# Second network in groups of 512 rows across experts, its outputs with channels on partitions

## The chip, the cores and the metric

The kernel runs on one core of a Trainium2 chip. The core has five engines with instruction streams of their own: TensorE (PE in the profile, matmuls), VectorE (DVE), ScalarE (ACT), GpSimd (POOL) and SyncE (SP, which issues most DMA transfers). They wait for each other by semaphores. The metric is the device time of one execution in microseconds; 707.64 before is the median of three runs (706.99 to 707.85).

## The reference

Three parts follow each other. Attention over 4 x 3072 positions with 256 channels gives 12288 rows. A mixture of experts sends each row to the one of eight experts with the highest gate, of which each takes at most `capacity` = 384 rows; the rest give zeros. A second network runs over all rows; the rows that no expert kept are zero going in and zero coming out, so only 8 x 384 = 3072 rows need it. The last two parts decide here:

```python
    h = np.maximum(np.einsum('ecd,edf->ecf', disp, w1), 0.0)   # 8 experts, 384 rows, 256 -> 1024
    y = np.einsum('ecf,efd->ecd', h, w2)                       # 1024 -> 256
    ...
            out[i] = gate_w[i] * y[expert_idx[i], pos[i]]
    ...
    h = x @ w_in                                               # 256 -> 2048
    g = np.where(h > 0.0, h, alpha * (np.exp(np.minimum(h, 0.0)) - 1.0))
    return (g @ w_out).astype(np.float32)                      # 2048 -> 256
```

## The kernel before

Every float32 product is made of three matmuls on rounded halves, high times high, low times high, high times low (`triples`, L127). A halving is one ACT instruction that rounds (`rounded`, L117) and one on DVE that takes the remainder (`rest`, L120). Weights of the experts come as raw float32 tiles of 1 MB, one for each layer of an expert (`load_w`, L145), and are halved in four pieces of 512 columns per layer (`split_w`, L231); a raw tile takes the next expert's load when its last piece is halved.

The experts' own network is `layer1` (L265, six matmuls of 384 columns for a tile of 128 hidden units, eight tiles), `hidden` (L277, ACT and DVE) and `layer2` (L286, six of 384). Expert 0 is done ahead of `feed_forward` (L1714). The second network then runs expert by expert: for expert e and each of 16 tiles f of 128 hidden units there is a step with `layer3` (six matmuls of 384), the ELU (class `Elu`: three ACT instructions at L1748 to L1750, two DVE sums at L1753 and L1756, then the halving) and `layer4` (three matmuls of 512 and three of 256, in which the activations are the stationary operand, so that the outputs come with rows on partitions, in three PSUM banks o0 to o2). After its 16 tiles, `finish` adds the two halves of each bank, and GpSimd writes the rows to their tokens.

PE, ACT, DVE and SP take their instructions in the order in which the code is written. In it `layer4` follows `layer3` by a lag of four products. The lag grows by one at six tiles of the last expert but one (`RAMP`), to ten, so that at the end PE has ten products to do while the last ELU is made. Layers 1 and 2 of expert n + 1 are placed among the 16 steps of expert n by the table `plan`, as are the weight halvings, loads, turns of the dispatched rows and zero fills. Expert 1's first layer1 comes right before the loop, the others in its steps 0 to 12, layer2 in its steps 4 to 13.

The ELU's tiles m, x and t have two buffers each, g three, the halves gh and gl ten. Dispatched rows come in "squares": 32 by 32 blocks, loaded in pieces of 128 bytes from DRAM so that DVE's 32 by 32 transpose gives whole turned tiles (`load_squares`, L178; `turn`, L236).

Of the kernel before, what the change touches and what calls it, by code (L numbers as in the profile page):

```python
# [19 lines left out]
P = 128  # L20
# [11 lines left out]
def tile_attn_moe_ffn(  # L32
# [28 lines left out]
    HALVED = 2  # L61
    assert D == 256 and E == 8 and DQ == 64 and cap % P == 0 and S % QA == 0
# [115 lines left out]
    def load_squares(e, to=None):  # L178

        if to is None:  # L180
            t = turns(1 + e % 2, 3, [P, ND, cap], F32, "squares")
            to = [t[:, d, :] for d in range(ND)]
# [18 lines left out]
    def load_toks(e):  # L201

        toks[e] = turns(1 + e % 3, 4, [P, CT, 1], F32, "toks")
# [32 lines left out]
    def turn(e, d, pool, to=None):  # L236
# [7 lines left out]
        else:  # L244
            t = to
            if t is None:
                t = pool.tile([P, cap], F32, tag="sq", name="sq", bufs=2)
# [29 lines left out]
    def hidden(e, f, ps):  # L277
        hi = hp.tile([P, cap], F32R, tag="hh", name="hh")
        lo = hp.tile([P, cap], F32R, tag="hl", name="hl")
# [1434 lines left out]
    def feed_forward(its, reach):  # L1714
        wp = its.enter_context(tc.tile_pool(name="wp", bufs=1))
        pools.append(its.enter_context(tc.tile_pool(name="dp2", bufs=1)))
        gp = its.enter_context(tc.tile_pool(name="gp", bufs=10))
        op = its.enter_context(tc.tile_pool(name="op", bufs=3))

        gs, os_ = {}, {}  # L1720

        def layer3(e, f):
            xh, xl = x2[e]
            ps = psum([P, cap], "h2")
            c = slice(f % 2 * P, (f % 2 + 1) * P)
            w = win[f // 2]
# [6 lines left out]
        class Elu:  # L1733

            def __init__(self, e, f, ps):
                self.ps = ps
                self.m, self.x, self.t = (
                    gp.tile([P, cap], F32, tag=n, name=n, bufs=2) for n in "mxt"  # L1740
                )
                self.g = gp.tile([P, cap], F32, tag="g", name="g", bufs=3)
                self.hi, self.lo = gs[e, f] = tuple(
                    gp.tile([P, cap], F32R, tag=n, name=n) for n in ("gh", "gl")
                )
# [6 lines left out]
            def sum(self):  # L1752
                nc.vector.scalar_tensor_tensor(  # L1753
                    out=self.t, in0=self.x, scalar=1.0, in1=self.t, op0=ALU.add, op1=ALU.mult
                )
                nc.vector.scalar_tensor_tensor(  # L1756
                    out=self.g, in0=self.ps, scalar=0.0, in1=self.t, op0=ALU.max, op1=ALU.add
                )

            def round(self):  # L1760
                rounded(self.hi, self.g)

            def rest(self):
                rest(self.lo, self.g, self.hi)

        def layer4(e, f, js=range(CT)):
            if f == 0:
# [22 lines left out]
        def finish(e, js=range(CT)):  # L1790
            for j in js:
                o = os_[e][j]
                t = op.tile([P, D], F32, tag="t", name="ot")
                nc.scalar.activation(out=t, in_=o[:, D:2 * D], func=ACTF.Copy)
                y = op.tile([P, D], F32, tag="y", name="oy")
                nc.vector.tensor_tensor(out=y, in0=o[:, 0:D], in1=t, op=ALU.add)  # L1796
                put = nc.gpsimd.indirect_dma_start(  # L1797
                    out=out[0:reach, :],
                    out_offset=bass.IndirectOffsetOnAxis(
                        ap=toks[e][:, j, :].bitcast(I32), axis=0  # L1800
                    ),
                    in_=y,
                    in_offset=None,
# [174 lines left out]
```

## Time and profile before

| | |
|---|---|
| profiled run | 707.44 us, its span 705.7 us |
| busy share of PE, DVE, ACT | 99%, 80%, 80% |
| granted TensorE clock, mean | 0.998 |
| second network with the layers of experts 1 to 7 | 314.2 to 700.5 us |
| last matmul, last output write issued | 700.13 us, 701.67 us |

Times in rows are microseconds from the start of the span, unless marked ns. A matmul's duration is longer than its distance to the next one, since matmuls are pipelined: distances from start to start give the throughput. The same holds for ACT and DVE where an instruction doesn't depend on the one ahead of it. "[0.21 <-PE h]" behind a row is idle time of that engine before it and what ended it.

### The profile page before, as it was taken

To read this page: it belongs to the slowest core of one execution; us is meant where nothing else is said; L and a number is where in the kernel's file an instruction comes from. 1 tells how busy PE (TensorE), PEld (TensorE's weight loads), DVE (VectorE), ACT (ScalarE), POOL (GpSimd) and SP (SyncE) were. 2 spreads that over 40 slices of the span, in tenths; PEclk is the share of its full clock that TensorE was granted. 3 is DMA by queue.
4 is the path that set the end of the run, shared out by engine and by line. 5 is a ranking of instruction groups with operands and counts; after the bars stand their busy time and mean duration, and the time that the engine had idled before them with its cause. 6 is when DMAs were issued, how large, how long until landed. Compare 5 with 4: busy or idle time off the path is not lost. (4 is left out here: it accounts for less than half of the span.)

```text
span 705.7 us, 11738 instructions
## 1 busy us (share of the span) xinstructions
PE 698.1 (99%) x3773; PEld 634.0 (90%) x3773; DVE 567.5 (80%) x1191; ACT 565.0 (80%) x1176; POOL 87.1 (12%) x143
## 2 busy tenths in 40 slices
PE   9999999999999999999999999999999999999997
PEld 6888888888888789999999999999999999999996
DVE  7879899898998968688797777777777777787782
ACT  7999989888775789759787777787777877787892
POOL 1003422303130201010001001001001001001011
PEclk9999999999999999999999999999999999999999
DMA  7878999989898864459821602603505406200000
GB/s 178 267 228 222 280 230 226 247 177 215 201 183 136 177 205 133 138 182 293 259 45 31 202 1 73 181 1 119 136 1 148 108 8 193 76 1 23 1 16 31
DMA packets 204595, 98.29 MB, mean 139 GB/s; under 512 B 158389, under 2 KB 193245, under 8 KB 204016
## 3 DMA queue, kind: packets, MB, share of 16 engines
q1 hardware_dynamic: 200016, 84.19, 47.1%
q0 software_dynamic: 4512, 13.31, 5.2%
q8 instruction: 30, 0.49, 0.3%
q14 instruction: 37, 0.30, 0.1%
HBM read 58.31 MB, written 38.03 MB: 137 GB/s over the span
## 5 line engine op out<-in xcount | busy, mean ns | idle before, releaser
L1778 PE MATMUL o<-wout,gh 128*128 128x512 f32 x384 | 139.2, 394 | 0.0
L1753 DVE SCALAR_TENSOR_TENSOR t<-x,t 128x384 f32<-128x384 f32 x128 | 71.5, 559 | 82.6 <-ACT t L1750 81.3
L1748 ACT ACTIVATE m<-h 128x384 f32<-128x384 f32 x128 | 62.7, 490 | 67.9 <-PE h L132 67.3
L1782 PE MATMUL o<-wout,gl 128*128 128x256 f32 x384 | 106.9, 280 | 0.0
L1130 ACT ACTIVATE own<-s 128x512 f32<-128x512 f32 (+1 forms) x123 | 68.4, 557 | 26.7 <-PE s L656 20.2
L129 PE MATMUL h<-xh,win 128*128 128x384 f32 x256 | 85.8, 335 | 0.0
L130 PE MATMUL h<-xh,win 128*128 128x384 f32 x256 | 85.5, 334 | 0.0
L1778 PEld LDWEIGHTS o<-wout,gh 128*128 128x128 f32 x384 | 71.8, 187 | 11.2
L1136 ACT ACTIVATE own<-own 128x512 f32<-128x512 f32 (+1 forms) x123 | 73.7, 599 | 2.7
L1756 DVE SCALAR_TENSOR_TENSOR g<-h,t 128x384 f32<-128x384 f32 x128 | 71.3, 557 | 4.4
L1782 PEld LDWEIGHTS o<-wout,gl 128*128 128x128 f32 x384 | 72.7, 189 | 0.2
L1749 ACT ACTIVATE x<-m 128x384 f32<-128x384 f32 x128 | 67.3, 526 | 4.1
L121 DVE TENSOR_TENSOR gl<-g,gh 128x384 fp32r<-128x384 f32 x128 | 69.9, 546 | 0.2 <-ACT gh L118 0.2
L118 ACT ACTIVATE gh<-g 128x384 fp32r<-128x384 f32 x128 | 65.2, 509 | 0.9 <-DVE g L1756 0.9
L132 PE MATMUL h<-xl,win 128*128 128x384 f32 x256 | 65.6, 337 | 0.0
L1750 ACT ACTIVATE t<-m 128x384 f32<-128x384 f32 x128 | 65.0, 508 | 0.0
L132 PE MATMUL acc<-ownr,vs 128*128 128x512 f32 (+1 forms) x204 | 59.0, 370 | 0.0
L1797 POOL DMA_INDIRECT out_dram<-oy,toks x21 | 21.4, 1020 | 295.8 <-DVE oy L1796 180.9
L129 PE MATMUL acc<-ownr,vs 128*128 128x512 f32 (+1 forms) x144 | 52.4, 367 | 0.0
L129 PEld LDWEIGHTS h<-xh,win 128*128 128x128 f32 x256 | 48.0, 188 | 4.7
L130 PE MATMUL acc<-ownr,vs 128*128 128x512 f32 (+1 forms) x144 | 51.8, 363 | 0.0
L130 PEld LDWEIGHTS h<-xh,win 128*128 128x128 f32 x256 | 48.0, 187 | 0.3
(169 smaller groups left out, 1704.1 us busy)
## 6 DMA issues: line engine op xcount, KB each, us to landing
raw<-in_moe_w_dram SPq DMA_DIRECT2D x16, 1024.0 KB
out_dram<-fill SPq DMA_DIRECT2D x32, 384.0 KB
own<-mir SPq DMA_DIRECT2D x180, 64.0 KB
mir<-own SPq DMA_DIRECT2D x36, 192.0 KB
vr<-in_v_dram SPq DMA_DIRECT2D x24, 256.0 KB
raw<-in_moe_w_in_dram SPq DMA_DIRECT2D x4, 1024.0 KB
raw<-in_moe_w_out_dram SPq DMA_DIRECT2D x4, 1024.0 KB
win<-win_d SPq DMA_DIRECT2D x8, 512.0 KB
```

Of the source, the lines that this page charges most:

```text
L118: nc.scalar.activation(out=out, in_=src, func=func)
L121: nc.vector.tensor_tensor(out=out, in0=src, in1=fp(hi), op=ALU.subtract)
L129: nc.tensor.matmul(out=ps, lhsT=hi, rhs=rh, start=first, stop=False)
L130: nc.tensor.matmul(out=ps, lhsT=lo, rhs=rh, start=False, stop=False)
L132: nc.tensor.matmul(out=ps, lhsT=hi, rhs=rl, start=False, stop=last)
L1130: nc.scalar.activation(out=s["a"][:, :nq], in_=s.pop("ps"), func=ACTF.Relu)
L1136: nc.scalar.activation(out=a, in_=a, func=ACTF.Square)
L1749: nc.scalar.activation(out=self.x, in_=self.m, func=ACTF.Exp, scale=-1.0)
L1753: nc.vector.scalar_tensor_tensor(out=self.t, in0=self.x, scalar=1.0, in1=self.t, op0=ALU.add, op1=ALU.mult)
L1756: nc.vector.scalar_tensor_tensor(out=self.g, in0=self.ps, scalar=0.0, in1=self.t, op0=ALU.max, op1=ALU.add)
L1778: both = lambda: nc.tensor.matmul(out=o, lhsT=hi[:, sl], rhs=w.rearrange("p a d -> p (a d)"), start=(f == 0), stop=(f == NF2 - 1),)
L1782: one = lambda: nc.tensor.matmul(out=o[:, 0:D], lhsT=lo[:, sl], rhs=w[:, 0, :], start=False, stop=False)
```

## The change

The 3072 rows are taken as six groups of 512, across the borders of experts, with 16 tiles each: 96 steps in place of 128. The input of the second network lies in a ring of 1536 columns (`xhr`, `xlr`) into which the outcome of every expert is halved (`settle`; `moved_on` copies expert 0's). `layer3` is six matmuls of 512. In groups 0 to 4 `layer4` is six matmuls of 512, with the weights stationary: outputs with channels on partitions, in one pair of PSUM banks, `ob`. After a group's last tile ACT copies one bank and DVE the other, two transfers write them to DRAM, sixteen read them back as squares, and six and seven steps later DVE turns them and GpSimd writes the rows out. The last group keeps the old form, with four banks.

Since the first group needs expert 1's rows too, expert 1's sixteen layers come before the first step, in a stretch of ten rounds. `layer2` of every expert now has its own bank pair, `yb`. Tiles m and t have one buffer, x three, gh and gl seven, squares one set instead of two. The ramp stands in the last group, at tiles 8, 10, 12 and 14, and uses the tiles of the halved expert weights, which are free by then. The table spreads layers 1 and 2 of experts 2 to 7 to ends at steps 11, 22.67, 34.33, 46, 62 and 78.

```diff
@@ -59,6 +59,8 @@
     CT = cap // P
     QA, QB, QC = 512, 320, 384
     HALVED = 2
+    GR, RING = 512, 4 * cap
+    GBUFS, LAG, RAMP = 7, 4, (8, 10, 12, 14)
...
@@ -1714,15 +1717,48 @@
     def feed_forward(its, reach):
         wp = its.enter_context(tc.tile_pool(name="wp", bufs=1))
         pools.append(its.enter_context(tc.tile_pool(name="dp2", bufs=1)))
-        gp = its.enter_context(tc.tile_pool(name="gp", bufs=10))
-        op = its.enter_context(tc.tile_pool(name="op", bufs=3))
-
-        gs, os_ = {}, {}
-
-        def layer3(e, f):
-            xh, xl = x2[e]
-            ps = psum([P, cap], "h2")
...
+        ring = tuple(xr.tile([P, ND, RING], F32R, name=n) for n in ("xhr", "xlr"))
+        yt, sqr = (
+            [xr.tile([P, 2 * D], F32, name=f"{n}{i}") for i in range(2)] for n in ("yt", "ysq")
+        )
+        back = [dram.tile([D, GR], F32, name=f"back{reach}{i}") for i in range(2)]
+        yb, ob = (
+            [ps_a.tile([P, GR], F32, tag=f"a{d}", name=f"{n}{d}") for d in range(ND)]
+            for n in ("yb", "ob")
+        )
+
...
+        def moved_on():
+            hi, lo = x_of(0)
+            nc.scalar.activation(out=hi, in_=fp(x2[0][0]), func=ACTF.Copy)
+            nc.vector.tensor_copy(out=lo, in_=fp(x2[0][1]))
+
+        def settle(e, ds=range(ND)):
+            hi, lo = x_of(e)
+            for d in ds:
+                split(hi[:, d, :], lo[:, d, :], ys[e][d])
+
+        def bank(e):
+            ys[e] = [t[:, 0:cap] for t in yb]
+
+        def held(e, f, ps):
+            hi, lo = (gp.tile([P, GR], F32R, tag=n, name=n)[:, 0:cap] for n in ("gh", "gl"))
+            hidden(e, f, ps, (hi, lo))
+
+        def layer3(g, f):
+            ps = psum([P, GR], "h2")
             c = slice(f % 2 * P, (f % 2 + 1) * P)
+            x = slice(g * GR % RING, g * GR % RING + GR)
+            xh, xl = (t[:, :, x] for t in ring)
             w = win[f // 2]
             triples(*(
                 (ps, w[:, 0, k, c], w[:, 1, k, c], xh[:, k, :], xl[:, k, :], k == 0, k == ND - 1)
...
-            def __init__(self, e, f, ps):
+            def __init__(self, g, f, ps):
                 self.ps = ps
                 self.m, self.x, self.t = (
-                    gp.tile([P, cap], F32, tag=n, name=n, bufs=2) for n in "mxt"
-                )
-                self.g = gp.tile([P, cap], F32, tag="g", name="g", bufs=3)
-                self.hi, self.lo = gs[e, f] = tuple(
-                    gp.tile([P, cap], F32R, tag=n, name=n) for n in ("gh", "gl")
-                )
+                    gp.tile([P, GR], F32, tag=n, name=n, bufs=b) for n, b in zip("mxt", (1, 3, 1))
+                )
+                if g == NG - 1 and f in RAMP:
+                    i = RAMP.index(f)
+                    t = fixed[("w1", "w2")[i // 2], i % 2].rearrange("p a b c -> p a (b c)")
+                    self.hi, self.lo = t[:, 0, :], t[:, 1, :]
+                else:
+                    self.hi, self.lo = (gp.tile([P, GR], F32R, tag=n, name=n) for n in ("gh", "gl"))
+                gs[g, f] = self.hi, self.lo
...
-        def layer4(e, f, js=range(CT)):
-            if f == 0:
-                os_[e] = [
-                    ps_a.tile([P, 2 * D], F32, tag="a0", name="o0"),
-                    ps_a.tile([P, 2 * D], F32, tag="a1", name="o1"),
-                    psum([P, 2 * D], "o2"),
-                ]
-            hi, lo = gs[e, f]
+                rest(self.lo, self.x, self.hi)
+
+        def layer4(g, f, js=range(GT)):
+            hi, lo = gs[g, f]
             w = wout[f // 2][:, f % 2]
+            if g < NG - 1:
+                for d in range(ND):
+                    c = slice(d * P, (d + 1) * P)
+                    triples((ob[d], w[:, 0, c], w[:, 1, c], hi, lo, f == 0, f == NF2 - 1))
+                return
             for j in js:
-                o = os_[e][j]
...
+        def columns_out(g):
+            nc.scalar.activation(out=yt[0], in_=ob[0], func=ACTF.Copy)
+            nc.vector.tensor_copy(out=yt[1], in_=ob[1])
+            to = back[g % 2]
+            for d in range(ND):
+                nc.sync.dma_start(out=to[d * P:(d + 1) * P, :], in_=yt[d])
+
+        def squares_in(g):
+            r = back[g % 2].rearrange("(k c) t -> c k t", c=SQ)
+            for j in range(GT):
+                t = sqr[j // 2][:, j % 2 * D:(j % 2 + 1) * D]
+                for s in range(0, P, SQ):
+                    nc.sync.dma_start(
+                        out=t[s:s + SQ].rearrange("p (k i) -> p k i", i=SQ),
+                        in_=r[:, :, j * P + s:j * P + s + SQ],
+                    )
+
+        def rows_out(g, i):
+            nc.vector.transpose(out=yt[i], in_=sqr[i])
+            for j in range(2):
+                put_out(GT * g + 2 * i + j, yt[i][:, j * D:(j + 1) * D])
...
-        RAMP = (1, 3, 5, 7, 9, 11)
-        FIRST1 = (-1, 0, 1, 5, 7, 9, 10, 12)
-        FIRST2 = (4, 5, 6, 8, 10, 11, 12, 13)
-        SPLIT1, SPLIT2 = (-1, -1, 3, 7), (0, 2, 6, 9)
+        def at(t, *step):
+            plan.setdefault(round(t), []).append(step)
+
...
+        ENDS = {2: 11, 3: 22.67, 4: 34.33, 5: 46, 6: 62, 7: 78}
+        for n, end in ENDS.items():
+            pace = (end - ENDS[n - 1]) / NF1 if n > 2 else end / (NF1 - 1)
+            l2 = [end - pace * (NF1 - 1 - s) for s in range(NF1)]
+            l1 = [t - 3 if n > 2 else max(t - 2, 0) for t in l2]
+            for s in range(NF1):
+                if n > 2 or s:
+                    at(l1[s], "layer1", n, s)
+                at(l2[s], "layer2", n, s)
...
-                at(e, 10 if one else 9, "load", n + 1, 1)
+                if n > 2 or q:
+                    at(max(l1[2 * q] - 3, 0) if q else l1[0] - 2, "split", n, 0, q)
+                    at(max(l2[2 * q] - 3, 0) if q else l2[0] - 2, "split", n, 1, q)
+            if n > 2:
+                for d in range(ND):
+                    at(l1[0] - 5 + 2 * d, "turn", n, d)
+                    at(l1[0] - 4 + 2 * d, "part", n, d)
+                at(max(l1[0] - 9, 0), "rows", n)
+            if n < E - 1:
+                at(l1[6] - 2, "load", n + 1, 0)
+                at(l2[6] - 2, "load", n + 1, 1)
...
-            for i in range(2, NP):
+            def load_tiles(i):
                 if i + 1 < NP:
...
+            split_w(1, 0, 1)
+            pick(2)
+            load_squares(2)
+            bank(1)
+            turns_ = {6: 0, 7: 1}
+            for f in range(NF1 + 2):
+                if f < NF1:
+                    held(1, f, layer1(1, f))
+                if f >= 4:
+                    layer2(1, f - 4)
+                for e, layer, q in {
+                    1: [(1, 0, 2)], 3: [(1, 0, 3), (1, 1, 0)], 5: [(1, 1, 1)], 6: [(1, 1, 2)],
+                    7: [(1, 1, 3)], 9: [(2, 0, 0)],
+                }.get(f, ()):
+                    split_w(e, layer, q)
+                if f == 0:
+                    moved_on()
+                if f == 4:
+                    load_w(2, 0)
+                    load_tiles(2)
+                if f in turns_:
+                    turn(2, turns_[f], gp)
+                    part(2, turns_[f])
+                if f == 8:
+                    load_w(2, 1)
+            for i in range(3, NP):
+                load_tiles(i)
...
+            for e in range(1, E):
+                load_toks(e)
+            for d in range(ND):
+                for f in (NF1 - 2, NF1 - 1):
+                    layer2(1, f, (d,))
+                settle(1, (d,))
+            hidden(2, 0, layer1(2, 0))
+            split_w(2, 1, 0)
...
+                    w()
+                products.append((g, f))
+                if g == NG - 1 and f in RAMP:
+                    lag += 1
+                if len(products) > lag:
+                    pg, pf = products.pop(0)
+                    layer4(pg, pf)
+                    if pf == NF2 - 1:
+                        columns_out(pg)
+                        squares_in(pg)
+                        for i in range(2):
+                            at(t + 6 + i, "put", pg, i)
+                        at(t + 8, "drain")
             for w in los + his + [last.rest]:
...
-            for j in range(CT):
+            for j in range(GT):
...
-                finish(E - 1, (j,))
+                finish(j)
```

Three places in the order of instructions follow. In the names, h1 and h2 are PSUM results of layer1 and layer3, hh and hl (or, in expert 1 after the change, gh and gl of 384) the halves of the experts' hidden values, w10 to w21 halved weight tiles (layer 1 or 2, two tiles each), raw0 and raw1 the raw weights, m, x, t and gh the ELU's.

ACT from the start of `feed_forward`, before:

```order
L118 ACTIVATE w11_3379<-raw0_126 128x512
L118 ACTIVATE hh_18620<-h10_18610 128x384
L1748 ACTIVATE m_18730<-h2_18717 128x384
L1749 ACTIVATE x_18731<-m_18730 128x384
L1750 ACTIVATE t_18732<-m_18730 128x384
L118 ACTIVATE hh_18741<-h11_18611 128x384
L118 ACTIVATE w20_3422<-raw1_127 128x512
```

and after:

```order
L120 ACTIVATE w10_3377<-raw0_126 128x512
L120 ACTIVATE gh_17771<-h1_17764 128x384
L120 ACTIVATE gh_17782<-h1_17775 128x384
L120 ACTIVATE w11_3379<-raw0_126 128x512
L120 ACTIVATE w20_3422<-raw1_127 128x512
L120 ACTIVATE gh_17797<-h1_17790 128x384
L120 ACTIVATE gh_17819<-h1_17812 128x384
```

Before, the first weights of layer2 (w20 from raw1) are rounded after the first ELU, some four steps ahead of layer2's first matmul. After, w20 stands behind the hidden values of layer1(1,3) and another weight piece, and layer2's first tile comes right after layer1(1,4).

PE at the last turn from one expert, or group, to the next, before:

```order
L1782 MATMUL o2_22738<-wout7_18665,gl_22946 128x256
L1778 MATMUL o2_22738<-wout7_18665,gh_22945 128x512
L129 MATMUL h2_23242<-xh1_19230,win5_18653 128x384
L130 MATMUL h2_23242<-xh1_19230,win5_18653 128x384
L129 MATMUL h2_23242<-xh1_19230,win5_18653 128x384
L130 MATMUL h2_23242<-xh1_19230,win5_18653 128x384
L132 MATMUL h2_23242<-xl1_19231,win5_18653 128x384 x2
L1778 MATMUL o0_23262<-wout0_181,gh_22971 128x512
L1782 MATMUL o0_23262<-wout0_181,gl_22972 128x256
L1778 MATMUL o1_23263<-wout0_181,gh_22971 128x512
```

and after (h2_21293 is layer3 of step 84):

```order
L131 MATMUL ob1_17714<-gh_21158,wout7_17910 128x512
L132 MATMUL ob1_17714<-gh_21158,wout7_17910 128x512
L134 MATMUL ob1_17714<-gl_21159,wout7_17910 128x512
L131 MATMUL h2_21293<-xhr_17703,win2_184 128x512
L132 MATMUL h2_21293<-xhr_17703,win2_184 128x512
L131 MATMUL h2_21293<-xhr_17703,win2_184 128x512
L132 MATMUL h2_21293<-xhr_17703,win2_184 128x512
L134 MATMUL h2_21293<-xlr_17704,win2_184 128x512 x2
L1814 MATMUL ob0_17713<-wout0_181,gh_21183 128x512
L1818 MATMUL ob0_17713<-wout0_181,gl_21184 128x256
L1814 MATMUL ob1_17714<-wout0_181,gh_21183 128x512
L1818 MATMUL ob1_17714<-wout0_181,gl_21184 128x256
```

Before, the next expert's outputs go to new banks (o0_23262). After, they go to the same ones, ob0 and ob1, and layer3 stands alone between the last product of group 4 and the first of group 5. The copies that empty the banks are on ACT behind the rounding of step 82 and on DVE behind the two sums of step 83:

```order
L1793 SCALAR_TENSOR_TENSOR x_21231<-h2_21223,x_21231 128x512
L123 TENSOR_TENSOR gl_21209<-x_21206,gh_21208 128x512
L1790 SCALAR_TENSOR_TENSOR x_21256<-x_21256,t_21257 128x512
L1793 SCALAR_TENSOR_TENSOR x_21256<-h2_21248,x_21256 128x512
L1851 COPY yt1_17706<-ob1_17714 128x512
```

DVE at the end of the network, before:

```order
L1756 SCALAR_TENSOR_TENSOR g_23359<-h2_23349,t_23358 128x384
L121 TENSOR_TENSOR gl_23335<-g_23333,gh_23334 128x384
L1753 SCALAR_TENSOR_TENSOR t_23384<-x_23383,t_23384 128x384
L1756 SCALAR_TENSOR_TENSOR g_23385<-h2_23375,t_23384 128x384
L121 TENSOR_TENSOR gl_23361<-g_23359,gh_23360 128x384
L121 TENSOR_TENSOR gl_23387<-g_23385,gh_23386 128x384
```

and after:

```order
L1793 SCALAR_TENSOR_TENSOR x_21556<-h2_21548,x_21556 128x512
L123 TENSOR_TENSOR gl_21532<-x_21529,gh_21531 128x512
L1790 SCALAR_TENSOR_TENSOR x_21573<-x_21573,t_21574 128x512
L1793 SCALAR_TENSOR_TENSOR x_21573<-h2_21565,x_21573 128x512
L123 TENSOR_TENSOR w21_3565<-x_21556,w21_3565 128x512
L123 TENSOR_TENSOR gl_21576<-x_21573,gh_21575 128x512
```

The order is the same: the remainder of the last product but one (gl_23361, w21) comes after the two sums of the last step. What moved is the ramp ahead of it. Before, its last step is some twenty steps ahead of these rows; after, steps 88 to 94 hold it, with DVE's turns of group 4's squares in steps 89 and 90 (`rows_out`).

## Rows read from the trace of the kernel before

**Rows 1.** First part of the page: busy us (share of span) and instruction count.

```profile
PE 698.1 (99%) x3773; PEld 634.0 (90%) x3773; DVE 567.5 (80%) x1191; ACT 565.0 (80%) x1176; POOL 87.1 (12%) x143
```

**Rows 2.** Busy time by stretch; header row gives the columns.

```profile
core 0: us, PE busy (x) PEld busy (x) DVE busy (x) ACT busy (x) POOL busy (x), PEclk, DMA share, GB/s
314.20:690.00 375.80, 375.80 (x2150) 360.66 (x2149) 288.59 (x558) 302.95 (x674) 21.79 (x21) 1.00 0.32 93
```

**Rows 3.** Timeline of PE in attention: start, duration, engine, line, operation; fourteen matmuls apart.

```profile
71.80 0.39 PE L129 MATMUL acc<-ownr,vs 128*128 128x512 f32 x1
...
74.97 0.39 PE L656 MATMUL s<-zs 128*128 128x512 f32 x1
```

**Rows 4.** Timeline of PE, one step: three pairs of layer4, six of layer3.

```profile
340.40 0.39 PE L1778 MATMUL o<-wout,gh 128*128 128x512 f32 x1
...
341.44 0.34 PE L129 MATMUL h<-xh,win 128*128 128x384 f32 x1
...
342.49 0.33 PE L129 MATMUL y<-hh,w 128*128 128x384 f32 x1
```

**Rows 5.** Timeline of ACT, one step of the last expert and the next one's start.

```profile
659.88 0.49 ACT L1748 ACTIVATE m<-h 128x384 f32<-128x384 f32 x1 [0.21 <-PE h L132]
660.41 0.53 ACT L1749 ACTIVATE x<-m 128x384 f32<-128x384 f32 x1
660.84 0.51 ACT L1750 ACTIVATE t<-m 128x384 f32<-128x384 f32 x1
661.25 0.51 ACT L118 ACTIVATE gh<-g 128x384 fp32r<-128x384 f32 x1
661.97 0.49 ACT L1748 ACTIVATE m<-h 128x384 f32<-128x384 f32 x1 [0.21 <-PE h L132]
```

**Rows 6.** Groups by line and shape, ACT: count, busy us and mean ns, idle before.

```profile
L1130 ACT ACTIVATE own<-s 128x512 f32<-128x512 f32 x99 | 58.1, 588 | 24.9 <-PE s L656 19.1 <-PE acc L132 3.0 <-DVE ownr L121 2.1
L118 ACT ACTIVATE w<-raw 128x512 fp32r<-128x512 f32 x63 | 39.0, 619 | 0.6 <-PE y L132 0.6
L118 ACT ACTIVATE hh<-h 128x384 fp32r<-128x384 f32 x64 | 30.4, 474 | 6.9 <-PE h L132 6.8
```

**Rows 7.** The same view, DVE.

```profile
L121 DVE TENSOR_TENSOR w<-raw,w 128x512 fp32r<-128x512 f32 x64 | 43.7, 682 | 0.2 <-ACT w L118 0.2
L1117 DVE STREAM_TRANSPOSE own<-own 128x512 f32<-128x512 f32 x45 | 30.9, 698 | 0.0
...
L732 DVE SCALAR_TENSOR_TENSOR ur<-acc,ur 128x512 f32<-128x512 f32 x12 | 7.8, 680 | 0.8 <-PE acc L132 0.8
...
L968 DVE CAST zs<-zps 128x512 fp32r<-128x512 f32 x3 | 2.1, 687 | 0.0
```

**Rows 8.** Timeline of SP, two 1 MB loads issued; then stretches with GB/s last.

```profile
306.17 3.72 SPq L148 DMA_DIRECT2D raw<-in_moe_w_dram  x2
...
306.20:310.70 4.50, 4.50 (x28) 4.50 (x27) 4.20 (x9) 1.62 (x3) 2.70 (x3) 1.00 0.69 238
310.70:314.20 3.50, 3.50 (x22) 3.50 (x22) 2.46 (x6) 2.33 (x5) 0.00 (x0) 1.00 1.03 328
```

**Rows 9.** Timeline of PE, ACT and DVE at the end of the network.

```profile
688.89 0.39 PE L1778 MATMUL o<-wout,gh 128*128 128x512 f32 x1
...
689.09 0.49 ACT L1748 ACTIVATE m<-h 128x384 f32<-128x384 f32 x1 [0.21 <-PE h L132]
...
691.65 0.55 DVE L121 TENSOR_TENSOR gl<-g,gh 128x384 fp32r<-128x384 f32 x1
...
692.95 0.28 PE L1782 MATMUL o<-wout,gl 128*128 128x256 f32 x1
...
700.13 0.39 PE L1778 MATMUL o<-wout,gh 128*128 128x512 f32 x1
```

**Rows 10.** Issues of squares by SP: one timeline row, and min/median/max ns by line.

```profile
317.15 4.42 SPq L186 DMA_DIRECT2D squares<-disp  x8
...
L186 SPq DMA_DIRECT2D squares<-disp x48: 316/742/2527, 317.1 to 554.2; - x48
```

More of the change, by code (lines that the diff above doesn't have):

```diff
@@ L201, in load_toks @@
     def load_toks(e):
[L203 removed]
+        toks[e] = turns(e, E, [P, CT, 1], F32, "toks")
         nc.sync.dma_start(
@@ L1788, in feed_forward @@
         puts = []
[L1790 to L1803, printed above, removed]
-                    bounds_check=reach - 1,
-                    oob_is_err=False,
-                )
-                if e == E - 1:
-                    for other in puts:
-                        tc.declare_no_dep(put.ins, other.ins, reason="a token's row is written once")
-                    puts.append(put)
@@ L1814, in feed_forward, with put_out @@
-        plan = {}
-        def at(e, f, *step):
-            plan.setdefault((e + f // NF2, f % NF2), []).append(step)
-        RAMP = (1, 3, 5, 7, 9, 11)
-        FIRST1 = (-1, 0, 1, 5, 7, 9, 10, 12)
-        FIRST2 = (4, 5, 6, 8, 10, 11, 12, 13)
-        SPLIT1, SPLIT2 = (-1, -1, 3, 7), (0, 2, 6, 9)
+        def put_out(b, y):
+            put = nc.gpsimd.indirect_dma_start(
+                out=out[0:reach, :],
+                out_offset=bass.IndirectOffsetOnAxis(
+                    ap=toks[b // CT][:, b % CT, :].bitcast(I32), axis=0
+                ),
+                in_=y,
+                in_offset=None,
+                bounds_check=reach - 1,
+                oob_is_err=False,
+            )
+            if b // GT == NG - 1:
+                for other in puts:
+                    tc.declare_no_dep(put.ins, other.ins, reason="a token's row is written once")
+                puts.append(put)
@@ L1859, in feed_forward @@
                     part(1, d)
-            load_toks(1)
-            spare = [ps_a.tile([P, cap], F32, tag=f"a{d}", name=f"h1{d}") for d in range(ND)]
-            split_w(1, 0, 1)
-            hidden(1, 0, layer1(1, 0, spare[0]))
-            for i in range(2, NP):
+            def load_tiles(i):
                 if i + 1 < NP:
@@ new lines, in feed_forward @@
+            for e in range(1, E):
[6 more added lines that the diff above has]
+            split_w(2, 1, 0)
+            his, los, last, products, lag = [], [], None, [], LAG
+            for t in range(NG * NF2):
+                g, f = t // NF2, t % NF2
+                ps = layer3(g, f)
+                first, later = [], []
+                for what, *args in plan.get(t, ()):
+                    if what == "layer1":
+                        first.append(partial(hidden, *args, layer1(*args)))
+                    elif what == "layer2":
+                        if args[1] == 0:
+                            bank(args[0])
+                        layer2(*args)
+                        if args[1] == NF1 - 1:
+                            later.append(partial(settle, args[0]))
+                    elif what == "turn":
+                        later.append(partial(turn, *args, gp))
+                    else:
+                        later.append(partial({
+                            "part": part, "split": split_w, "rows": load_squares, "zero": zero,
+                            "halve": split_wout, "load": load_w, "squares": squares_in,
+                            "put": rows_out, "drain": lambda: tc.keep_in_program_order(nc.gpsimd.drain()),
+                        }[what], *args))
+                elu = Elu(g, f, ps)
+                elu.exp()
+                for w in los:
+                    w()
+                elu.sum()
+                for w in his + first:
+                    w()
+                los = [last.rest] if last else []
+                his = [elu.round]
+                last = elu
+                for w in later:
+                    w()
+                products.append((g, f))
[10 more added lines that the diff above has]
+                        at(t + 8, "drain")
```

114 lines of the change are left out of this document (28 added, 86 removed).

## Prediction

> **What bounds the kernel now.** I read the busy shares first: PE is busy for 99% of the span, DVE and ACT for 80% each [rows 1]. A share says nothing about one stage, so I then cut out the stretch that the change touches, 314.2 to 690 us. There PE's 2150 matmuls fill all of the 375.8 us, at a granted clock of 1.00 [rows 2], the upper of its two levels, and the waits of PE in this stretch are an empty list. So here the time is the sum of the matmul steps, and only two things can move it: cheaper matmuls, or a wait that PE doesn't have yet. ACT and DVE have spare time and matter only where PE catches up with them. The profiled run took 707.44 us, 0.2 below the median of 707.64. I sum against the profiled run and add 0.2 at the end.
>
> **What the wider groups remove.** The second network has the same columns before and after: 128 steps of 12 matmuls with 4608 columns (six of 384, three of 512, three of 256), and then 96 steps with 6144, both 589,824. The matmul count falls from 1536 to 80 x 12 + 16 x 14 = 1184, by 352. So the gain is what a matmul costs whatever its width. Fourteen matmuls of 512 take 74.97 - 71.80 = 3.17 us, 0.2265 each [rows 3]. A step of before shows three pairs of 512 and 256 in 1.04 and six of 384 in 1.05 [rows 4]; ACT's first instruction recurs every 2.09 [rows 5]. At 1.00 of 2.4 GHz, 512 columns are 0.2133, so 13 ns of the 0.2265 are fixed. Before: 128 x 2.087 = 267.1. After: 80 x 12 x 0.227 = 217.9, and 16 x (6 x 0.227 + 4 x 0.348) = 44.1, the sum 262.0. **Saving 5.1.** Bounds: the 256, 384 and 512 of the network's own steps also fit a price proportional to columns (0.117, 0.175, 0.232), which would save nothing; with all of the fixed part at its largest, 352 x 16 ns is 5.6. I take the rows of 512 themselves, in this kernel and with the same operand form.
>
> The Trainium skill, "TensorE: Matmul & The Clock Gate", section "Wait — 56ns, not 53.3ns?", gives warm back-to-back matmuls as columns over 2.4 GHz plus about 2.5 ns. By that page the saving would be 352 x 2.5 ns = 0.9 us, an estimate. The trace differs, with 13 ns here.
>
> **ACT and DVE in a group step.** A 384 step gives ACT 0.53, 0.43, 0.41, 0.41 [rows 5]. Going from 384 to 512 adds 0.10 (0.490 against 0.588 reading PSUM) [rows 5, 6]. So a 512 step is 0.61 + 0.54 + 0.52 + 0.52 = 2.2 us, less than PE's 2.73. DVE needs two of 0.71 (0.680 long [rows 7], one waiting for the other) and 0.60 for the remainder, 2.0. PE's end reaches ACT after 0.20 (688.89 to 689.09) [rows 9]; I use 0.04 from ACT to DVE and 0.08 back to PE. In the middle I find ACT and DVE ahead: weight splits stand two or three steps before their use, and at the group turns at steps 19, 35, 51 and 67 one layer1 or layer2 (1.05 each) lies between the last product and the first one into the same banks. I cost these, the 5 x 16 square loads and the DVE transposes of the first four turns at nothing. This cover goes if a square load outlasts six steps (16 us).
>
> **Five new waits of PE, each walked from the order.**
> *A, first layer2 of expert 1.* It needs the split of its weights, which ACT does after hidden(1,3) and another split, as the order shows. From the end of layer1(1,3): 0.20, hidden 0.37 (0.474 long [rows 6], of which the next one covers 0.10, as 0.51 long at 0.41 apart in [rows 5]), a split 0.62 and 0.04, then on DVE the two remainders, 0.60 and 0.68, and 0.08, in all 2.6 (0.619 and 0.682 are [rows 6, 7]; the second split on ACT runs beside the first remainder). PE has only layer1(1,4) and one matmul to do, 1.05 + 0.17. **+1.4.** Before, some four steps of the network lay between.
> *B, layer2(2,0) in the first step.* Its 1 MB load can only be issued when the split of (1,1,3) has freed the raw tile, 1.54 after layer2(1,3), plus 0.2. Two such loads were issued at 306.17 and 309.52, and the bytes moved (238 x 4.5 = 1.07 MB, 328 x 3.5 = 1.15 MB) put their landing near 310.7 and 313.9 [rows 8], so 4.5 each. Then a split, 1.42. Sum 7.7; PE has five layers of 1.05, layer3's 1.36 and 0.17, together 6.8. **+0.9**, from 0.5 to 2 with the landing.
> *C, layer1(2,2) in step 1.* Its split stands behind the first group's three ACT instructions, which B has made late, and hidden(2,1): **+0.5.**
> *D, the last turn, steps 83 to 84.* ACT copies the one bank, DVE the other after the two sums of step 83; with T the end of layer3(83) they are free at T + 0.20 + 2.2 + 0.59 + 0.06 = 3.05 and at T + 3.4 + 0.69 = 4.07 (copy 0.687 [rows 7]). PE wants them at T + 2.73 and 0.35 later. No layer1 or layer2 is left to cover. **+1.0.** Before, the next expert had other banks.
> *E, the tail.* The ramp that saves up products now stands in the last group: in steps 88, 90, 92 and 94 PE does layer3 alone, so two steps take PE 1.36 + 2.76 = 4.12 and ACT 4.4. ACT falls behind. From the end of layer3(88): ACT reaches relu(95) after 0.21 + 7 x 2.2 = 15.6; its three instructions 1.8, two DVE sums 1.4 and the remainder of product 94, 0.6, bring 19.4, while PE has done layer3(95), a product of 1.39 and seven at 0.348 by 17.4. The two transposes (0.70 each [rows 7]) in steps 89 and 90 add up to 0.4. **+2.2**, from 1.5 to 3. Before, the ramp lay in the expert before the last and ACT had caught up: the remainder at 691.65 is done 0.75 ahead of its matmul at 692.95 [rows 9]. After the last matmul (700.13 [rows 9]) the work is the same.
>
> **Sum.** 707.44 - 5.1 + 1.4 + 0.9 + 0.5 + 1.0 + 2.2 = 708.3; with 0.2 for the median, 708.5.
>
> **Rivals.** *R1, the waits are smaller than walked.* Each is a difference of two long chains, and a few tenths in ACT's hand-over or a faster landing empties A to C; if the ramp's steps also leave ACT level, E goes. For it: before has no PE wait at all at similar handovers. Against it: A and D follow from order alone. With a third to none of 6.0 left, 702.5 to 704.5, and faster.
> *R2, the DRAM turn is late.* Of a 1 MB load's 4.5 us, 3.2 go to its bytes at 328 GB/s [rows 8], so 1.3 remain; I give a store or a square load, of far fewer bytes, 2 us. The squares of group 4 then start 4.1 + 0.4 + 2 = 6.5 after the end of layer3(83). Sixteen issues at 0.55 (eight in 4.42) or at the median 0.742 [rows 10] take 8.8 or 11.9, and with landing the last are there after 17.3 or 20.4; DVE reaches its second transpose after 19.6. The margin is 2.3 us or -0.8. If the squares need over 2 us more than the middle of these, DVE stands before the transpose, ACT's tanh behind DVE (one t tile), and all of it reaches the tail: +3 to 4, 711.5 to 712.5, slower. The Trainium skill, "DMA: Bandwidth & Descriptors", section "Specifications", names 512 bytes as the least for the line rate; these pieces are 128. The trace shows squares in such pieces, issued as above, but doesn't show a turn through DRAM.
> *R3, the fixed price is not there.* If the network's matmuls cost by columns, or 2.5 ns each, the saving is 0 to 0.9 and the waits stay: 712.5, slower. For it speaks only that the step's own three widths fit a straight line through zero; against it, fourteen matmuls in a row [rows 3].
>
> **How the numbers follow.** A measurement of this kernel can tell about 0.2%, 1.4 us: faster means under 706.2, slower over 709.1. Forecast 0.55, its own range 706.5 to 710 from the bounds of B and E (of it 0.04 faster, 0.38 the same, 0.13 slower). R1 0.18, R2 0.16, R3 0.06; the remaining 0.05 is spread (0.01, 0.03, 0.01). Faster 0.23, same 0.41, slower 0.36. For 8 in 10 the range takes in most of R1 and of R2: 704.5 to 711.8.
>
> **What would show it.** Matmuls of 512 in the group steps at 0.227 from start to start, and some 262 us for the network's own: the saving. PE idle of 1.4 before the first layer2 of expert 1, released by DVE's split; 0.9 and 0.5 in the next two steps; none from step 2 to 82; 1.0 at the turn to the last group, ended by the two copies; 2.2 in the tail ahead of the remainder of product 94. Squares that land before the transpose begins: R2 wrong. It is wrong if PE idles in the middle, or if no idle shows at the start.

## The result and the profile after

The changed kernel takes 713.69 us (median of four runs, 713.19 to 714.48) against 707.62, a ratio of 1.0088 with an interval of 1.0071 to 1.0106. It is slower by 6.1 us, where the forecast was 708.5 and the range ended at 711.8. Its profiled run took 713.46, with a span of 711.7.

First the busy shares, as in [rows 1], then PE by stretch, as in [rows 2], with the same columns.

```profile
PE 699.0 (98%) x3421; PEld 598.0 (84%) x3421; DVE 558.5 (78%) x1091; ACT 546.1 (77%) x1034; POOL 88.2 (12%) x143
```

```profile
core 0: us, PE busy (x) PEld busy (x) DVE busy (x) ACT busy (x) POOL busy (x), PEclk, DMA share, GB/s
314.20:340.00 25.80, 23.48 (x126) 21.58 (x124) 16.80 (x30) 15.05 (x30) 0.00 (x0) 1.00 0.64 214
...
400.00:500.00 100.00, 100.00 (x479) 87.11 (x479) 72.01 (x120) 72.92 (x138) 4.29 (x4) 1.00 0.38 104
...
680.00:700.00 20.00, 18.70 (x94) 15.34 (x93) 17.32 (x27) 16.23 (x30) 4.64 (x4) 1.00 0.07 27
```

PE has 352 matmuls fewer and is busy 0.9 us longer. Idle time is where it was forecast, at the start and at the end, and in the middle there is none. The waits of PE from 314 us on, an empty list before (columns: who waited for whom, us in total, times, longest):

```profile
PE yb L131 <- ACT w L120: 1.7, 2, 1.1
PE ob L1818 <- DVE w L123: 1.0, 1, 1.0
PE yb L132 <- DVE w L123: 0.6, 2, 0.4
PE ob L1814 <- DVE yt L1851: 0.4, 1, 0.4
PE ob L1814 <- ACT w L120: 0.3, 1, 0.3
PE h L132 <- DVE w L123: 0.3, 1, 0.3
```

This list sums to 4.3 us, but less than a wait costs: a matmul that had to wait stands with 0.44 to 0.50 us in the records where one of its form in a row has 0.34 to 0.39, so part of the wait hides in its duration. Start-to-start distances don't have this flaw. I therefore split the way from the first layer1 of expert 1 to the last matmul (314.17 to 700.13 before, 313.83 to 706.13 after) into distances of the usual size for their width and what is over it:

| | before | after |
|---|---|---|
| 384 columns | 1440 x 175.1 ns | 672 x 174.6 ns |
| 512 columns | 383 x 232.1 ns | 1119 x 232.6 ns |
| 256 columns | 384 x 117.1 ns | 64 x 118.2 ns |
| sum of matmuls | 385.96 us | 385.15 us |
| over it (waits) | 0 | 7.14 us |

So the matmuls gained 0.8 us in place of 5.1, and the waits took 7.1 in place of 6.0. Together the stretch is 6.3 longer; the run of after came to its start 0.3 earlier, with the same work ahead of it, and so the two ends differ by 6.0.

The price of 512 columns is seen in any step without layers 1 and 2. PE of after, two rows twelve matmuls of 512 apart:

```profile
424.01 0.40 PE L131 MATMUL h<-xhr,win 128*128 128x512 f32 x1
...
426.81 0.40 PE L131 MATMUL h<-xhr,win 128*128 128x512 f32 x1
```

2.80 / 12 = 233 ns, against 226.5 in attention before the change [rows 3] and 227.1 in the attention of this kernel, the mean of its distances up to 300 us, at the same granted clock of 1.00.

Wait A, at layer2's first tile of expert 1. PE, then ACT and DVE:

```profile
318.74 0.51 PE L134 MATMUL h<-dl,w 128*128 128x384 f32 x2
319.82 0.45 PE L131 MATMUL yb<-gh,w 128*128 128x384 f32 x1 [0.57 <-ACT w L120]
320.62 0.44 PE L132 MATMUL yb<-gh,w 128*128 128x384 f32 x1 [0.36 <-DVE w L123]
320.91 0.34 PE L131 MATMUL yb<-gh,w 128*128 128x384 f32 x1
...
318.62 1.14 ACT L120 ACTIVATE w<-raw 128x512 fp32r<-128x512 f32 x2
...
319.28 1.29 DVE L123 TENSOR_TENSOR w<-raw,w 128x512 fp32r<-128x512 f32 x2
```

The row of 318.74 holds two matmuls, so the next one was due at 319.09; it starts 0.73 late. The one behind it starts 0.80 later in place of 0.17, since it needs the second remainder of the pair on DVE. With 0.11 on the third this is 1.47, against 1.4 forecast, and the chain is the one that was walked: both splits stand behind the hidden values on ACT.

Wait B, at layer2(2,0). SP issues the load; ACT waits for it; PE waits for ACT and DVE:

```profile
329.52 0.38 SPq L150 DMA_DIRECT2D raw<-in_moe_w_dram  x1
329.95 0.58 SPq L312 DMA_DIRECT2D win<-win_d  x1
...
335.05 0.63 ACT L120 ACTIVATE w<-raw 128x512 fp32r<-128x512 f32 x1 [1.27 <-DMA raw<-in_moe_w_dram]
...
335.73 0.44 PE L131 MATMUL yb<-hh,w 128*128 128x384 f32 x1 [1.10 <-ACT w L120]
336.45 0.44 PE L132 MATMUL yb<-hh,w 128*128 128x384 f32 x1 [0.28 <-DVE w L123]
```

From issue to ACT's start it is 5.5 us, not the 4.5 of [rows 8]. SP issues nine more loads behind it, four `win` tiles of 512 KB and five of `wout` of 256 KB, the first of them 0.43 us later. Behind the two loads of [rows 8] the next issue came 3.4 and 3.1 us later. In these 5.53 us the DMA engines moved 253 GB/s, 1.40 MB, so some 0.35 MB of it belonged to other loads. B costs 1.9, C behind it 0.53.

Wait D, at the turn to the last group (PE and DVE), and wait E, in the tail (DVE and PE):

```profile
666.18 0.68 DVE L1851 COPY yt<-ob 128x512 f32<-128x512 f32 x1
...
666.91 0.50 PE L1814 MATMUL ob<-wout,gh 128*128 128x512 f32 x1 [0.43 <-DVE yt L1851]
...
696.07 0.69 DVE L1793 SCALAR_TENSOR_TENSOR x<-h,x 128x512 f32<-128x512 f32 x1
696.67 0.68 DVE L123 TENSOR_TENSOR w<-x,w 128x512 fp32r<-128x512 f32 x1
...
697.41 0.38 PE L1818 MATMUL ob<-wout,w 128*128 128x256 f32 x1 [1.03 <-DVE w L123]
```

D measures 1.10 over both banks and E 1.92 (0.51 on the rounded half, 1.30 on the remainder of product 94, 0.11 after). A further 0.21 at 383 us was not forecast.

The turn through DRAM is not late. SP issues the last squares, and DVE comes to its transposes without a wait:

```profile
668.97 7.72 SPq L1861 DMA_DIRECT2D ysq<-back  x16
...
683.47 0.70 DVE L1867 STREAM_TRANSPOSE yt<-ysq 128x512 f32<-128x512 f32 x1
...
685.99 0.70 DVE L1867 STREAM_TRANSPOSE yt<-ysq 128x512 f32<-128x512 f32 x1
```

The last is issued by 676.7, 6.8 us ahead of the first transpose: an issue took 0.48 in the mean, not 0.55 to 0.74.

### The profile page after: what moved, and what is told of

Read it like the earlier page. It is cut to its first block, busy times and chain, and to the rows that moved or that the text cites. A ratio compares the mean times of both kernels' runs of the same rounds, so it can differ in the third digit from the quotient of the medians.

```text
span 711.7 us, 11105 instructions
## 1 busy us (share of the span) xinstructions
PE 699.0 (98%) x3421; PEld 598.0 (84%) x3421; DVE 558.5 (78%) x1091; ACT 546.1 (77%) x1034; POOL 88.2 (12%) x143
## 5 line engine op out<-in xcount | busy, mean ns | idle before, releaser
L1790 DVE SCALAR_TENSOR_TENSOR x<-x,t 128x512 f32<-128x512 f32 x96 | 66.4, 692 | 91.5 <-ACT t L1787 91.2
L1785 ACT ACTIVATE m<-h 128x512 f32<-128x512 f32 x96 | 57.3, 597 | 83.2 <-PE h L134 82.9
L132 PE MATMUL h<-xhr,win 128*128 128x512 f32 x192 | 76.0, 396 | 0.0
L131 PE MATMUL h<-xhr,win 128*128 128x512 f32 x192 | 75.8, 395 | 0.0
L1793 DVE SCALAR_TENSOR_TENSOR x<-h,x 128x512 f32<-128x512 f32 x96 | 66.4, 691 | 3.3
L134 PE MATMUL ob<-gl,wout 128*128 128x512 f32 x160 | 63.5, 397 | 0.0
L1786 ACT ACTIVATE x<-m 128x512 f32<-128x512 f32 x96 | 60.7, 632 | 3.1
L131 PE MATMUL ob<-gh,wout 128*128 128x512 f32 x160 | 62.9, 393 | 0.0
L132 PE MATMUL ob<-gh,wout 128*128 128x512 f32 x160 | 62.8, 392 | 0.0
L123 DVE TENSOR_TENSOR gl<-x,gh 128x512 fp32r<-128x512 f32 x92 | 62.2, 676 | 0.1
L134 PE MATMUL h<-xlr,win 128*128 128x512 f32 x192 | 60.3, 396 | 0.0
L1787 ACT ACTIVATE t<-m 128x512 f32<-128x512 f32 x96 | 59.1, 616 | 0.0
```

The costliest lines, as they stand in the source:

```text
L123: nc.vector.tensor_tensor(out=out, in0=src, in1=fp(hi), op=ALU.subtract)
L131: nc.tensor.matmul(out=ps, lhsT=hi, rhs=rh, start=first, stop=False)
L132: nc.tensor.matmul(out=ps, lhsT=lo, rhs=rh, start=False, stop=False)
L134: nc.tensor.matmul(out=ps, lhsT=hi, rhs=rl, start=False, stop=last)
L1785: nc.scalar.activation(out=self.m, in_=self.ps, func=ACTF.Relu, scale=-1.0)
L1786: nc.scalar.activation(out=self.x, in_=self.m, func=ACTF.Exp, scale=-1.0)
```

## Experiments

Two questions were open: whether the waits are what they seem, and why 512 columns cost 5.6 ns more here than in attention. "Price" is the mean start-to-start distance of 512-column matmuls from 314 us on, waits left out, and "stretch" the way from the first layer1 of expert 1 to the last matmul, 385.96 us before and 392.30 after. Where no ratio is given, the time is that of one run. The runs were made on four chips, on which the kernel before took 707.7 (e1 to e3), 707.4 (e4 to e7), 708.6 (e8 to e10) and 709.3 (e11, one run), so between chips the price and the stretch are safer to compare than the time.

### The waits taken away

```diff
+    GROW = (0, 4, 6, 8, 10)
...
-            pace = (end - ENDS[n - 1]) / NF1 if n > 2 else end / (NF1 - 1)
+            pace = (end - ENDS[n - 1]) / NF1 if n > 2 else (end - 2) / (NF1 - 1)
...
+                if n == 2 and q == 0:
+                    at(0, "split", n, 1, q)
...
-                    1: [(1, 0, 2)], 3: [(1, 0, 3), (1, 1, 0)], 5: [(1, 1, 1)], 6: [(1, 1, 2)],
+                    1: [(1, 0, 2)], 2: [(1, 1, 0)], 3: [(1, 0, 3)], 5: [(1, 1, 1)], 6: [(1, 1, 2)],
...
-            split_w(2, 1, 0)
...
-                if g == NG - 1 and f in RAMP:
+                if g == NG - 1 and f in GROW:
```

> The changed kernel with the five waits taken away: the first layer-2 split of expert 1 two rounds earlier (A), layer2 of expert 2 from step 2 on and its first split inside step 0 (B, C), the lag growing at tiles 0, 4, 6, 8 and 10 of the last group in place of 8, 10, 12 and 14 (D: a step without a product lies behind the last turn; E: ACT has five steps to catch up and nine products wait at the end). The gaps between matmuls measured in the changed kernel are A 1.5, B 1.9, C 0.5, D 1.1, E 1.9, sum 7.1 with 0.2 elsewhere. My theory now (the waits were sized about right, and the saving of 5.1 is missing because 512 columns cost 232.6 ns here): 713.7 - 6.5 = 707.2, that is the kernel before again, within 1 us. Rival (waits only move the bound on, ACT or DVE becomes late elsewhere): over 709.

The edit for A moves that split by one round, not two: from round 3, where it stood behind another split, to round 2. Measured (e3_waits): 707.97 against 707.74 for the kernel before, ratio 1.0004 (0.9995 to 1.0014), the same time. The waits over matmul sums fell from 7.1 to 1.1 us, and in PE's list of waits one is left:

```profile
PE ob L1815 <- DVE yt L1852: 0.2, 1, 0.2
```

The price stayed at 232.6 ns. So the five waits are some 6 us, the whole of the loss, and without them the wide groups still give nothing, as the price says.

### Is it the data?

```diff
-            nc.scalar.activation(out=hi, in_=fp(x2[0][0]), func=ACTF.Copy)
+            nc.scalar.activation(out=hi, in_=fp(x2[0][0]), func=ACTF.Copy, scale=0.0)
```

and so in `settle`; the low halves become high minus high. The weights keep their values.

> The changed kernel with the second network's input set to zero: the two halves in the ring are written with scale 0, so layer3, the ELU and layer4 multiply zeros (their output is left out of the computation); every instruction, shape and wait stays. In the trace of the changed kernel a 512-column matmul of the network takes 232.6 ns from start to start, in attention 227. Theory 'data' (the extra 5.6 ns hang on the values that are multiplied): the network's 512 fall to 227, about 1000 of them, time 713.5 - 5 to 6 = 708. Theory 'address' (they hang on where the operands lie): still 232.6, 713.5. Theory 'place' (anything else in this stage, for instance the other engines' traffic): still 232.6, 713.5.

e1_zero_x: 713.28, price 232.6. Twelve matmuls of zeros, from one layer3 to the next:

```profile
423.83 0.40 PE L131 MATMUL h<-xhr,win 128*128 128x512 f32 x1
...
426.63 0.40 PE L131 MATMUL h<-xhr,win 128*128 128x512 f32 x1
```

2.80 again. The values of the rows play no part.

### Is it the place of the operands?

An address here is the byte at which the built program places a tile within a partition. One unused tile ahead of the ELU's tiles moves these, gh and gl among them, the ring and what follows:

```diff
+        gp.tile([P, 8], F32, tag="pad", name="padg", bufs=1)
         NG, GT = NSLOT // GR, GR // P
```

> The changed kernel with one unused tile of 32 bytes ahead of the ELU's tiles, so that gh, gl and the ring of inputs lie 32 bytes further on: moving and stationary operands of the network then have the same address modulo 128, as they have in attention (before this edit 64 against 96). Theory 'address': 512-column matmuls of the network at 227 ns in place of 232.6, time about 708. Theories 'data' and 'place': no change, 713.5.

e2_shift32: 710.98, price 229.0. A step as above, now 2.73 for twelve, 227.5 each:

```profile
423.32 0.39 PE L131 MATMUL h<-xhr,win 128*128 128x512 f32 x1
...
426.05 0.39 PE L131 MATMUL h<-xhr,win 128*128 128x512 f32 x1
```

> The changed kernel with an unused tile of 288 bytes in place of the 32 of e2_shift32: gh, gl and the ring then have the same address as the weights modulo 512 too (96), as all operands in attention. In e2_shift32 layer3 fell to about 228 ns a matmul, layer4 to 230 with 224 to 240 by position. Theory 'equal modulo 512': all at 227, and by that 2 us less than e2_shift32 without its slow stretch in the tail, about 707. Theory 'equal modulo 64 is all that counts': the same pattern as e2_shift32, matmuls 229.0 on average.

e5_shift288: 711.38, price 229.0, the same pattern: like modulo 512 brings no more than like modulo 64. The stretches of the two, 389.76 and 389.78, are alike too; both lost some 1.6 us to a lower clock in the tail (last section).

> The changed kernel with 32 bytes ahead of the first pool and 32 ahead of the ELU's tiles: attention's operands and the network's all lie at a multiple of 64 bytes, the network's weights, ring, gh and gl at 0 modulo 128. Theory 'like against unlike': attention stays at 227 ns for 512 columns and the network is at 227 to 229. Rival ('32 past a multiple of 64 is the good place'): attention rises to 232 too, with 1100 such matmuls some 6 us more, and the network stays at 232.

e6_all: 709.87, price 229.0, stretch 388.09, and attention's matmuls at 227.3 after 227.1. So it isn't one good place; it is that the operands agree.

> The changed kernel with an unused tile of 96 bytes ahead of the ELU's tiles: gh, gl and the ring lie at 32 modulo 128, the weights at 96. Theory 'like modulo 64 is enough': 512-column matmuls of the network at 229.0 ns as in e2_shift32, e5_shift288 and e6_all. Theory 'like modulo 128': back at 232.6 ns.

e8_shift96: price 229.6, but 714.28. Here ring, gh and gl differ from the weights modulo 128 and agree modulo 64, which is enough for the 512. The stretch is 391.47: the 512 save 3.4 us, but 1.4 went to a lower clock after wait B (last section), and the 384 of layer2 rose from 175.2 to 177.1 ns, which was not explained. The time is longer than the changed kernel's all the same, since this run came to the stretch 1.6 us later, at 315.45, with the same work ahead of it.

> Control for the shifts: the changed kernel with an unused tile of 64 bytes ahead of the ELU's tiles, so that gh, gl and the ring lie at 0 modulo 128 and the weights at 96, still unlike modulo 64. Theory 'like modulo 64': 512-column matmuls at 232.6 ns as in the changed kernel, about 713.5. Rival (any other place than the first one helps): 229 to 230.

e11_shift64: price 232.9, 715.18 beside 709.29 for the kernel before on the same chip, stretch 393.13. Twelve matmuls:

```profile
425.22 0.40 PE L131 MATMUL h<-xhr,win 128*128 128x512 f32 x1
...
428.02 0.40 PE L131 MATMUL h<-xhr,win 128*128 128x512 f32 x1
```

Six arrangements now divide by one property: ring, gh and gl 64 or 0 against weights at 96 (modulo 128, unlike modulo 64): 232.6 and 232.9. At 96 against 96 (twice), 0 against 0, 32 against 96 (like modulo 64): 229.0 to 229.6. Layer3 alone goes from 233.2 to some 228 (229 in e8_shift96), layer4 from 232 to 230 with some positions still at 236 to 240. So like addresses take away 3.6 of the 5.6 ns over attention's price; the other 2 are unexplained. Every shift moves the ELU's other tiles along, which no run separates.

### The same shift in the kernel before

> The kernel before with one unused tile of 32 bytes ahead of the ELU's tiles, so that the halves gh and gl, the stationary operands of layer4, lie at 96 modulo 128 like the moving w_out (64 against 96 without it). In the trace of before a 512-column matmul of layer4 takes 232.1 ns from start to start, a 256-column one 117.1. Theory 'address' (unlike addresses modulo 64 cost some 5 ns in a matmul of 512): 383 x up to 5 ns = 1.9 us, 707.7 - 1 to 2 = 706. Rival (only the moving operand or the ring's place counts): 707.7, no change.

e4_before_shift32 is a miss: 708.61 against 707.39, ratio 1.0016 (1.0005 to 1.0026), slower. The 512 fell to 230.1 ns, but the 256 rose from 117.1 to 120.0 and the 384 from 175.1 to 175.8: 384 x (2.9 - 2.0) + 1440 x 0.7 ns = 1.35 us, about what was measured. So agreement modulo 64 isn't a rule that makes every stream of matmuls faster; with widths of 384, 512 and 256 by turns it cost time.

### The turn left out

```diff
                     if pf == NF2 - 1:
-                        columns_out(pg)
-                        squares_in(pg)
-                        for i in range(2):
-                            at(t + 6 + i, "put", pg, i)
-                        at(t + 8, "drain")
+                        pass
```

> The changed kernel without the turn through DRAM: the copies out of the banks, the stores, the square loads, the DVE transposes and the row writes of groups 0 to 4 are left out (their rows of the output are not written). My theory: the turn costs PE only what D is (1.1 us) and 0.2 to 0.4 of E through the transposes in steps 89 and 90; 713.5 - 1.1 to 1.5 = 712.2. Rival (the turn's transfers and DVE work cost more, also in the matmuls): under 711.

e10_no_turn: PE's waits fall from 7.14 to 6.05 us: D is gone and E is 0.1 smaller; the price is 232.6 as before. So on PE the turn costs 1.1 to 1.2 us. The stretch, 391.16, is shorter by as much. The run itself took 715.86, a miss, since from the last matmul to the end of the span it needs 8.6 us where the changed kernel needs 5.6. The row writes are not late: the last packet of the last one moves at 709.0, in the changed kernel at 709.7. What is longer is GpSimd's drain at the end of the program, 4.7 us (708.51 to 713.24) in place of 2.7 (707.62 to 710.31). The edit also left out the five earlier drains, one behind each turn; that this is the reason was not tried. The time says nothing on the turn.

### Both causes taken away

> e3_waits and e5_shift288 together: the five waits gone and the operands' addresses equal modulo 512. If both causes are as I now hold, 707.97 - 4 = 704, faster than the kernel before by 0.5%. If the address counts for nothing without the waits (the matmuls then being held by something else), 707.5 to 708.

e7_waits_shift: 704.27 against 707.39, ratio 0.9962 (0.9950 to 0.9975): both kernels beaten. Waits 1.3 us, price 229.0. The stretch is 381.92, so the matmuls alone take 380.7 where before they took 385.96. The 5.3 us are near the 5.1 of the forecast, but by other prices: 512 columns at 229.0 and not 227, and the 384 of layers 1 and 2 at 173.8, in the changed kernel 174.6. The largest wait left, 0.64, stood at the last turn. The next edit moves the copies there:

```diff
                 elu.exp()
+                if g == NG - 1 and products and products[0] == (g - 1, NF2 - 1) and len(products) >= lag:
+                    products.append((g, f))
+                    pg, pf = products.pop(0)
+                    layer4(pg, pf)
+                    columns_out(pg)
                 for w in los:
                     w()
                 elu.sum()
...
```

> e7_waits_shift with the copies out of group 4's banks ahead of the ELU's sums on DVE and ahead of the rounding on ACT (in e7_waits_shift PE still waits 0.64 us there). If the order of the copies is the cause, 0.5 us less than e7_waits_shift: 703.7. If not, 704.3 as before.

e9_turn_early: 703.75 against 708.6 on its chip, ratio 0.9941 (0.9924 to 0.9957). That the time meets the forecast of 703.7 is chance, since this chip runs the kernel before 1.2 us slower than that of e7_waits_shift; the stretch, 381.24, is 0.7 shorter than that of e7_waits_shift, where 0.5 was forecast. The wait at the turn is gone, 0.7 us of waits are left in all, and the start is full:

```profile
314.20:340.00 25.80, 25.80 (x141) 24.43 (x140) 18.52 (x34) 18.32 (x36) 0.00 (x0) 1.00 0.74 235
...
660.00:690.00 30.00, 30.00 (x154) 25.35 (x153) 25.12 (x40) 24.83 (x46) 5.07 (x5) 1.00 0.20 51
```

## Why the prediction was wrong, by its steps

**The saving was the step that failed.** The term of 5.1 measured 0.8. That is 4.3 of the 5.2 us between the forecast of 708.5 and the 713.7 measured, and made of a time within noise of before a slower one; the rest is about 1.1 more of waits, less the 0.3 by which the run came to the stretch earlier. I took 0.227 for a matmul of 512 from attention [rows 3], though the network's own steps held 384 of them. [Rows 4] gave only pairs of 512 and 256, and at attention's price the 256 of a pair of 0.348 would take 0.121. The rows between, from the same step of before, part the two:

```profile
340.40 0.39 PE L1778 MATMUL o<-wout,gh 128*128 128x512 f32 x1
340.63 0.28 PE L1782 MATMUL o<-wout,gl 128*128 128x256 f32 x1
340.75 0.40 PE L1778 MATMUL o<-wout,gh 128*128 128x512 f32 x1
```

From start to start that is 0.23 and 0.12; over all steps it is 232.1 and 117.1 ns. The second bound, a price by columns, fitted the three widths of the very stage that was to change, and I gave it 0.06 because it had to be wrong in attention. It needn't hold there: the price is not one number in this kernel. The forecast for this rival, 712.5, was the nearest of all, and its sum was a little low: 707.44 less a saving of 0 to 0.9, with 6.0 of waits and the 0.2 for the median, is 712.7 to 713.6.

What made the price differ is shown in part: the operands' addresses (e2, e5, e6, e8, e11), not the values (e1). That the traffic of other engines is not needed for it is argued, not tried: in the tail after 700 us, where ACT and DVE are busy 1.2 and 1.3 us of 6.5, the 512 distances are still 230.8. Why unlike addresses cost time, why layer4 keeps 230 and why the kernel before got slower by the same edit stays open.

The figure of the Trainium skill ("TensorE: Matmul & The Clock Gate", section "Wait — 56ns, not 53.3ns?") that stood beside the sum, 2.5 ns a matmul and a saving of 0.9, is nearly the measured 0.8, but not for its reason: attention's 512 kept 13 ns over their columns, the network's 19, so in neither stage is it 2.5 here.

**A, C, D, E** were right in place, mechanism and size: 1.47, 0.53, 1.10 and 1.92 against 1.4, 0.5, 1.0 and 2.2, and with all five removed the time came back (e3). The transposes' part of E, up to 0.4 in the forecast, was 0.1 (e10). **B** was right in mechanism and 1.0 too small: the landing took 5.5 us where 4.5 was taken from two loads that had almost nothing issued behind them until 3 us later. The 0.35 MB that other loads moved meanwhile would be 1.1 us at the 328 GB/s of [rows 8], an estimate that fits; no run took those loads away. The stretch from step 2 to 82 was forecast without waits and has 0.21.

**R1** fell: the waits were not smaller. **R2** fell: the squares were issued 6.8 us ahead. **R3** was it, with the waits.

The answer was to be had from the rows: ACT's first instruction recurs every 2.09 us [rows 5], 2.087 over four steps, which is 4608 columns, and by columns 6144 take 2.783; 128 steps of the one and 96 of the other are 267 us both.

## What to carry to other kernels

Take a price from the stage that changes, by start-to-start distances of each form there, and if two laws fit the rows, weigh them by how near their rows are and not by how clean one of them is; here a price from another stage of the same kernel was 2.5% off, and that was the whole gain. When a PE-bound kernel is rearranged, walk the chains that lose their cover: four of five waits were found to 0.3 us from the order and the rows. Here the wider tiles won only when the new seams (first layer2, last turn, tail) were covered again and the operands' places were changed: with both the same change went from 0.9% slower to 0.4% faster, and to 0.6% with the copies at the last turn moved too.

## What the runs showed of the hardware beyond that

Matmul prices that hang on operand addresses modulo 64 bytes, by 1.5% of a 512-column matmul (232.6 against 229.0 ns), were not expected, nor that the same shift can cost time when widths alternate (256 columns from 117.1 to 120.0).

The clock can turn a wait into more. In e2_shift32 and e5_shift288 the tail's wait of 1.3 us was followed by some 3 us at a granted clock of 0.50 to 0.52, the lower of its two levels, though PE was busy all through it again; in the changed kernel, e1, e6, e10 and e11 the same wait was not. Windows of the changed kernel around that wait (PEclk is the third column from the end):

```profile
695.40:697.50 2.10, 0.80 (x4) 0.28 (x3) 1.97 (x4) 1.05 (x2) 0.00 (x0) 1.00 0.10 35
697.50:700.00 2.50, 2.50 (x15) 2.24 (x16) 0.65 (x1) 0.00 (x0) 0.00 (x0) 1.00 0.00 0
```

and of e2_shift32:

```profile
691.00:694.00 3.00, 1.70 (x5) 1.00 (x5) 2.70 (x5) 1.36 (x3) 0.00 (x0) 0.91 0.12 44
694.00:697.00 3.00, 3.00 (x11) 2.57 (x10) 0.06 (x1) 0.00 (x0) 0.00 (x0) 0.52 0.00 0
697.00:700.00 3.00, 3.00 (x19) 2.59 (x18) 0.85 (x2) 0.77 (x2) 0.98 (x1) 1.00 0.00 0
```

and of e8_shift96 after wait B:

```profile
338.50:341.70 3.20, 3.20 (x11) 3.20 (x11) 1.38 (x2) 0.61 (x2) 0.00 (x0) 0.50 1.04 385
```

These stretched distances cost some 1.7 us in e2_shift32, 1.6 in e5_shift288 and 1.4 in e8_shift96. So of two kernels with the same wait one pays more than the wait, and the single times hide it: without the lower clock e2_shift32 would stand near 709.3 and e5_shift288 near 709.8. What decides whether the clock falls, these runs don't show.
